# A turn's small matmul tiles in one cluster, with TensorE's program aligned to its fetch blocks

## The chip, the cores and the metric

The kernel runs on one core of one Trainium2 chip. The metric is the device time of one execution in microseconds; lower is better.

## What is computed

A gated linear attention is followed by a gated state-space block. With B=4, H=8, S=768, D=48:

```python
for t in range(S):
    state = alpha[:, :, t, :, None] * state + np.einsum('bhd,bhe->bhde', k[:, :, t], v[:, :, t])
    y[:, :, t] = np.einsum('bhd,bhde->bhe', q[:, :, t], state)
x = y.transpose(0, 2, 1, 3).reshape(B, S, H * D)          # (4, 768, 384)
proj = x @ w_in                                            # w_in: (384, 1024)
val, gate = proj[..., :512], proj[..., 512:]
for t in range(S):
    h = exp(A_log) * h + val[:, t, :]
    ys[:, t, :] = h
out = (silu(gate) * ys) @ w_out                            # w_out: (512, 384)
```

Everything is computed in float32; `w_in`, `A_log` and `w_out` come as float64.

## The kernel before

The 3072 rows are cut into 12 chunks of 256, three for each batch. A turn n projects chunk n and does its output while the attention of chunk m = n+1 is finished and that of chunk m+1 is begun. The program order of each engine is written out by hand in the loop over n; there is no scheduler behind it, and every engine works its list in order. Turns 0 and 1 are special; from n=2 on the turns are alike.

The attention of a chunk has these parts. VectorE turns alpha, k and q (`turn`, L601), scans alpha to running products P and V (L636, L655), and scales k and q with them to `Zk` and `Zq` (L620, L611). These are the steps of `products`; `go(1)` issues the next one, and seven belong to a chunk. TensorE then works in tiles of 48 or 64 rows, four side by side: `scores` (L799) multiplies Zk and Zq; `masks` (L814, L815, L819, L821) takes the results out to `A0`, `AK` and `K0` with VectorE, ScalarE and GpSimd; `values(m, True)` and `values(m, False)` (L835) multiply v with the masked scores across and within 64-row halves; `states` (L867) makes each half's addition to the state, which ScalarE evicts to `dS` (L875) and GpSimd adds up to `sums` (L887, `add_up`); and `carried` (L848) multiplies q with the sums. `third` is carried, values and carried again, and `join` copies the result `y` to `yst` and `xT` (ScalarE, L961, L962, L967) and moves the pieces that change partitions with DMAs from SyncE and GpSimd (L964).

A float32 matmul shows as two passes of TensorE, each with a weight load of its own. A projection (`project`, L989) is six matmuls, so twelve passes, of 128x256 with full 128-row tiles; four of them make the 48 passes of a turn. Its first half feeds a scan on VectorE (L996), its second half a SiLU on ScalarE (L1007), and GpSimd multiplies both (L1009). The output (`output_parts`, L1072) uses a Strassen-like form with seven half-width products, 28 passes of 128x192; it is a generator, whose pieces the loop draws with `next(outs)`. Its sums of inputs are S1 to S4 (L1056 to L1061), and VectorE's three additions of results (L1100 to L1102) are its last piece, which the following turn draws.

PSUM has eight banks. Two pairs have names, s and y; the other four are taken in the order of a string of digits, `taken`, written by hand (`bank`). There is one buffer each for raw alpha, k and q: the load of the next chunk waits until the present one is turned. `check_w` looks at the exponents of the weights; its result, with other conditions, chooses at the end between the fast kernel and a general one, by a branch on every engine.

In a turn from n=3 on TensorE's order before is: four projections; `carried`, `values(m, False)`, `carried`; `scores(m+1)`; the output's 28 passes; `values(m+1, True)`, `states(m+1)`; the next turn's projections. The outer ones are large tiles, the others small.

Of the kernel before, what the change touches and what calls it, by code (L numbers as in the profile page):

```python
# [343 lines left out]
FLOOR = 1e-31  # L344


@with_exitstack
def fast(
# [128 lines left out]
    As, Ks = [A0, AK[:, :, :, D:]], [K0, AK[:, :, :, 0:L]]  # L477
# [184 lines left out]
    def products(m):  # L662
# [21 lines left out]
                 "23012301" "230132" "01230123" "012310" "23012301" "230132" "01230123" "012310"  # L684
                 "23012301" "230132" "01230123" "012310" "23012301" "230132" "01230123" "012310"
                 "23012301" "0132" "01320132" "0132")

    def bank(tag=None):
        if tag:
            return ps_at.tile([C, 512], FP32, tag=tag, name=tag)  # L690
        return ps_mm.tile([C, 512], FP32, tag=f"mm{next(taken)}", name="mm")
# [111 lines left out]
    def masks(m, cs=range(G), between=None):  # L803
# [9 lines left out]
        for c in range(G):  # L813
            nc.vector.tensor_mul(A0[:, c], sc[c][0][:, :, D:], mb.to_broadcast([C, 4, L]))  # L814
            nc.scalar.activation(AK[:, c], sc[c][1], AF.Copy)  # L815
        if between:
            between()
        t = AK.rearrange("p c h x -> p (c h) x")[:, :, D:]
        nc.gpsimd.tensor_mul(t, t, mb.to_broadcast([C, G * 4, L]))  # L819
        for c in range(G):  # L820
            nc.scalar.activation(K0[:, c, :, 0:D], sc[c][0][:, :, 0:D], AF.Copy)  # L821

    def values(m, across):

        v_sb = vs[m % NV]
        if across:
            ys[m] = [t.rearrange("p (e t) -> p e t", e=2) for t in bank_pair("y")]
        for c in range(G):
            for e in range(2):
                for h in range(2):  # L830
                    i = 1 - h if across else h
                    for s in range(2):
# [3 lines left out]
                                         v_sb[rows, c, 4 * i + p, :], As[i][rows, c, p, :],  # L836
# [15 lines left out]
    def states(m):  # L852
# [7 lines left out]
        for c in range(G):  # L860
            for p in range(4):
                for h in range(2):
                    if c < n[h]:
                        rows = ds(L * h, L)
                        for i in range(2):
                            to = st[h][ds(64 * i, D), c, p, :] if m else st[h][c][ds(64 * i, D), p, :]
                            nc.tensor.matmul(to, ((K0, dS[m % 2][1]) if m < NG else Ks)[i][rows, c, p, 0:D],  # L867
# [6 lines left out]
        for h in range(2):  # L874
            nc.scalar.activation(parts[h][:, 0:n[h], :, 0:D], st[h][:, 0:n[h]], AF.Copy)  # L875
# [100 lines left out]
    def project(n, cc, late=False, between=None):  # L976
# [14 lines left out]

        passes(order[:NK] if between else order)
# [82 lines left out]
    def output_parts(n):  # L1075
# [11 lines left out]
        yield  # L1087
# [125 lines left out]
    def second(m):  # L1213
        if m < N:
            values(m, True)
            states(m)
            add_up(m, (0, 1, 2))

    def third(m):
        if m < N:  # L1220
            carried(m, (1,))
            values(m, False)
            carried(m, (0, 2, 3))
            return join(m, [nc.sync, nc.gpsimd])

    late = (1,)
    for n in range(N):
# [37 lines left out]
        elif n == 1:  # L1265
# [29 lines left out]
            f2()  # L1295
            output(0)
# [8 lines left out]
        else:  # L1305
            if n == 2:
                first(m)
            if n - 1 not in late:
                go(1)
                if n == N - 2:  # L1310
                    check_w(5)
                next(outs, None)
                second(m)
                go(1)
                if n == N - 2:
                    check_w(0)
            else:
                go(1)
            f0 = project(n, 0)
            f0()  # L1320
            if n == N - 2:
                check_w(1)
            if n == 2:
                go(1)
            load_raw("a", n + 3, nc.sync)
            load_raw("k", n + 3, nc.sync)
            if n != 2:
                go(1)
# [3 lines left out]
            if n - 1 in late:  # L1332
                second(m)
            if n == 2:
                go(1)
# [10 lines left out]
            load_raw("q", n + 3, nc.sync)  # L1346
# [3 lines left out]
            f3 = project(n, 3)  # L1350
            f3()
            if m + 1 < N:
                go(1)
# [6 lines left out]
            rest = third(m)  # L1360
            if n < N - 1:
                outs = output_parts(n)
# [25 lines left out]
        if n == N - 2:  # L1388
            for _ in outs:
                pass  # L1390
# [55 lines left out]
```

## Time and profile before

| | us |
|---|---|
| median of 3 runs | 269.65 (269.63 to 269.8) |
| the profiled execution | 269.61 |
| its span, first to last instruction | 267.9 |
| TensorE (PE) busy | 262.4 |
| VectorE (DVE) busy | 236.9 |
| GpSimd (POOL) busy | 166.0 |
| ScalarE (ACT) busy | 111.9 |

PE are the matmul passes, PEld the weight loads that overlap them. In the chain of waits each line has its start, its length and the work, with the count of passes; ends of matmuls are modelled, so the border between two pieces stands a little behind the start of the next piece's first pass. In a timeline a bracket at the end of a line gives the engine's idle time before it and what ended it. In a stretch of time the columns are its length, then the busy time of PE, PEld, DVE, ACT and POOL with their instructions, the granted clock, the DMA share and GB/s. TensorE's granted clock is 1.00 throughout.

### The profile page before, as it was taken

Reading aid. Unit: us, or ns where it says so; the run is one execution under the profiler, and the core shown is the slowest. Engines: PE = TensorE matmul, PEld = TensorE weight load, DVE = VectorE, ACT = ScalarE, POOL = GpSimd, SP = SyncE. Lnnn points to the kernel's source line nnn. Section 1 sums busy time; section 2 is a strip of 40 time slices with the busy share of each in tenths; the row PEclk is TensorE's granted clock in tenths of the full one; section 3 lists DMA queues with packets and bytes.
Section 4 is the critical chain, followed back from the end, with each engine's and each line's share of the span. In section 5 each row is a group of like instructions: output and inputs, shape, how many; then the busy total and the mean of one; then the engine's idle time right before and its main releaser. Section 6 shows DMA issues by size and latency. Waiting matters only on the chain.

```text
span 267.9 us, 10005 instructions
## 1 busy us (share of the span) xinstructions
PE 262.4 (98%) x4172; PEld 230.5 (86%) x4172; DVE 236.9 (88%) x326; ACT 111.9 (42%) x272; POOL 166.0 (62%) x186
## 2 busy tenths in 40 slices
PE   7999999999999999999999999999999999999994
PEld 5998889877688988988988988988988989988984
DVE  7979998996999999999999998999999998883462
ACT  4667766372242642532533524524524515214021
POOL 8221314084168997995985995996876986646010
PEclk9999999999999999999999999999999999999999
DMA  5948984896993669559697488569598501201101
GB/s 177 307 141 262 287 187 152 227 209 149 271 219 82 133 164 223 122 146 221 132 230 165 104 218 184 125 160 216 128 209 174 144 2 29 76 2 38 68 7 60
DMA packets 52304, 41.19 MB, mean 154 GB/s; under 512 B 27392, under 2 KB 50944, under 8 KB 52256
## 3 DMA queue, kind: packets, MB, share of 16 engines
q1 hardware_dynamic: 49472, 37.53, 57.8%
q0 software_dynamic: 1536, 2.20, 3.2%
q10 hardware_dynamic: 1248, 0.79, 1.1%
q8 instruction: 34, 0.56, 0.9%
q14 instruction: 14, 0.11, 0.1%
HBM read 32.54 MB, written 4.72 MB: 139 GB/s over the span
## 4 chain that ended last, share of the span: by engine, by line
PE 91%; DVE 2%; DMA 2%; issue 1%; ACT 1%; POOL 1%; ACTq 0%; DVEq 0%; POOLq 0%
PE mm L989 47%; PE mm L1072 18%; PE y L835 4%; PE y L848 4%; PE mm L1023 4%; PE s L799 4%; PE mm L799 3%; PE s L867 3%; DMA raw_q<-in_q_dram 2%; PE mm L708 1%; PE mm L704 1%; PE mm L703 1%; DVE P L636 1%; PE mm L751 1%; POOL w_in L557 1%
## 5 line engine op out<-in xcount | busy, mean ns | idle before, releaser
L989 PE MATMUL mm<-xT,w_in 128*128 128x256 f32 x576 | 129.2, 382 | 0.1
L989 PEld LDWEIGHTS mm<-xT,w_in 128*128 128x128 f32 x576 | 108.0, 190 | 15.8 <-POOL w_in L557 0.4
L1007 ACT ACTIVATE sg<-mm 128x256 f32<-128x256 f32 x48 | 18.4, 383 | 88.8 <-PE mm L989 84.4
L1009 POOL TENSOR_TENSOR f_last<-sg,hh 128x256 f32<-128x256 f32 x36 | 28.3, 794 | 26.1 <-ACT sg L1007 22.6
L887 POOL TENSOR_TENSOR sum<-sum,dS 128x192 f32<-128x192 f32 x30 | 39.7, 1325 | 3.0 <-ACT dS L875 1.4
L636 DVE TENSOR_TENSOR_SCAN P<-al,lower 128x1028 f32<-128x1028 f32 x12 | 30.7, 2562 | 0.3
L996 DVE TENSOR_TENSOR_SCAN hh<-a_dec,hh,mm 128x256 f32<-128x256 f32 x32 | 23.3, 729 | 8.3 <-PE mm L989 7.8
L655 DVE TENSOR_TENSOR_SCAN V<-al,ends 128x1028 f32<-128x1028 f32 x12 | 28.5, 2375 | 0.4
L964 POOL DMA_DIRECT2D xT<-yst x44 | 22.5, 517 | 5.1 <-ACT yst L961 3.7
L557 POOL TENSOR_TENSOR w_in<-w_in,wr 128x768 int32<-128x768 int32 x4 | 7.3, 1823 | 25.5 <-DVE wr L552 16.1
L1072 PE MATMUL mm<-wide,wr 128*128 128x192 f32 x120 | 23.0, 327 | 0.0
L1072 PEld LDWEIGHTS mm<-wide,wr 128*128 128x128 f32 x120 | 20.0, 190 | 0.0
L601 DVE STREAM_TRANSPOSE k<-raw_k 128x1024 f32<-128x1024 f32 x9 | 18.5, 2054 | 0.0
L601 DVE STREAM_TRANSPOSE q<-raw_q 128x1024 f32<-128x1024 f32 x9 | 18.3, 2030 | 0.0
L875 ACT ACTIVATE dS<-s 128x384 f32<-128x384 f32 (+1 forms) x18 | 7.4, 461 | 24.4 <-PE s L867 24.4
L1072 PE MATMUL mm<-w_out,f_last 128*128 128x192 f32 x80 | 17.4, 340 | 0.0
L819 POOL TENSOR_TENSOR AK<-AK,mask 128x512 f32<-128x512 f32 x9 | 13.7, 1522 | 5.9 <-ACT AK L815 5.7
L601 DVE STREAM_TRANSPOSE al<-raw_a 128x1024 f32<-128x1024 f32 x8 | 16.4, 2052 | 0.0
L620 DVE TENSOR_TENSOR Zk<-k,V 128x1024 f32<-128x1024 f32 (+1 forms) x14 | 16.0, 1146 | 0.3 <-ACT k L715 0.3
L611 DVE TENSOR_TENSOR Zq<-q,P 128x1024 f32<-128x1024 f32 (+1 forms) x14 | 15.7, 1120 | 0.0
L848 PEld LDWEIGHTS y<-Zq,sum 48*64 48x64 f32 x656 | 11.6, 134 | 3.5 <-issue 3.2
L835 PE MATMUL y<-A,v 64*64 64x64 f32 x352 | 14.5, 221 | 0.0
(196 smaller groups left out, 502.5 us busy)
## 6 DMA issues: line engine op xcount, KB each, us to landing
out_dram<-o_sb SPq DMA_DIRECT2D x23, 192.0 KB, 2.3
v<-in_v_dram SPq DMA_DIRECT2D x22, 192.0 KB, 4.1
raw_k<-in_k_dram SPq DMA_DIRECT2D x18, 184.0 KB, 5.2
raw_q<-in_q_dram SPq DMA_DIRECT2D x18, 184.0 KB, 5.4
raw_k<-in_k_dram SPq DMA_DIRECT2D x18, 176.0 KB, 5.4
raw_q<-in_q_dram SPq DMA_DIRECT2D x18, 176.0 KB, 5.4
wbits<-in_moe_w_in_dram SPq DMA_DIRECT2D x8, 384.0 KB, 4.9
raw_a<-in_alpha_dram SPq DMA_DIRECT2D x16, 184.0 KB, 3.9
```

The costliest lines, as they stand in the source:

```text
L601: nc.vector.transpose(out=by_runs(to).rearrange("p h c j -> p h j c"), in_=raws[name][:, 0:4 * ROW].rearrange("p (h j d) -> p h j d", h=4, ...
L636: nc.vector.tensor_tensor_scan(out=P, data0=al[:, 0:4 * GP], data1=lower.rearrange("p h t -> p (h t)"), initial=0.0, op0=ALU.mult, op1=ALU ...
L655: nc.vector.tensor_tensor_scan(out=V[:, ::-1], data0=al[:, 1:4 * GP + 1][:, ::-1], data1=ends.rearrange("p h t -> p (h t)")[:, ::-1], init ...
L799: nc.tensor.matmul(scs[m][c][i][ds(L * h, L), ds(p * (L + D), L + D)], Zk[rows, c, p, ds(h * L, L)], Zq[rows, u, p], start=True, stop=True ...
L835: nc.tensor.matmul(ys[m][i][ds(64 * s, 64), e, ds(c * C + h * L, L)], v_sb[rows, c, 4 * i + p, :], As[i][rows, c, p, :], start=across and ...
L848: nc.tensor.matmul(ys[m][i][ds(64 * s, 64), e, ds(u * L, L)], Ss[j][rows, p, :], Zqs[m % 2][rows, u, p, D:], start=False, stop=True, skip_ ...
L887: nc.gpsimd.tensor_add(Ss[j][:, :, 0:D], Ss[j - 1][:, :, 0:D], part)
L964: engines[n % len(engines)].dma_start(out=xT[to, a], in_=st[rows, i, e])
L989: nc.tensor.matmul((pv, pg)[vg], w_ins[cc][:, kk, vg, :], xT[:, kk, :], start=(kk == 0), stop=(kk == NK - 1))
L996: nc.vector.tensor_tensor_scan(out=hh, data0=a_dec[:, cc:cc + 1].to_broadcast([C, GC]), data1=pv, initial=prev_h[cc][:, GC - 1:GC] if n % ...
L1009: f = lambda: engine.tensor_mul(fs[n][cc], sg, hh)
L1072: nc.tensor.matmul(o, a[:, k], b[k] if type(b) is list else b[:, k], start=start and k == 0, stop=k == KC - 1, skip_group_check=True)
```

## The change

`scores(m+1)` moves directly behind the last projection, ahead of `carried`. `states(m+1)` and `values(m+1, True)` move from behind the output to directly behind `carried`, so that a turn has one cluster of small tiles instead of two; for m in `apart` (5 and 8), they stay behind the output. Because the y tiles of two chunks now overlap, those after the first batch's take rotating banks (the string has the letters a and b for the named y banks too), and `A0` and `AK` get second buffers in the place of the finished weight bits `wobits[0]`, whose check moves into turn 1; another check moves to the end of turn 9. GpSimd's mask is done in two halves. The eviction of states becomes a function called between pieces of the output. The steps of `products` shift by one place in the turn, the last scan and gate of a turn come behind the scaled q, and the raw loads move. Ahead of the third projection in turns 2 to 9 `addr_align(256, BLOCK_PLACE, max_nops=0)` places the next TensorE instruction at slot 212 of a block of 256 program slots of 64 bytes; the padding is jumped over by a branch.

```diff
+BLOCK_PLACE = 212
...
-    As, Ks = [A0, AK[:, :, :, D:]], [K0, AK[:, :, :, 0:L]]
+    spare_A = wobits[0].rearrange("p a n two -> p (a n two)").bitcast(FP32)
+    AKs = [spare_A[:, 0:G * 4 * (D + L)].rearrange("p (c h x) -> p c h x", c=G, h=4), AK]
+    A0s = [spare_A[:, ds(G * 4 * (D + L), G * 4 * L)].rearrange("p (c h x) -> p c h x", c=G, h=4), A0]
...
-                 "23012301" "230132" "01230123" "012310" "23012301" "230132" "01230123" "012310"
-                 "23012301" "230132" "01230123" "012310" "23012301" "230132" "01230123" "012310"
-                 "23012301" "0132" "01320132" "0132")
+                 "23012301" "23" "01" "23ba" "23ab23ab" "23" "ab" "2310"
+                 "23012301" "23" "23ba" "01" "23ab23ab" "23" "ab" "2310"
+                 "23012301" "23" "01" "23ba" "23ab23ab" "23" "2310" "ab"
+                 "23012301" "23" "01" "23ba" "23ab23ab" "23" "ab" "2310"
+                 "23012301" "2310" "23ab01ab" "0132")
...
         for c in range(G):
-            nc.vector.tensor_mul(A0[:, c], sc[c][0][:, :, D:], mb.to_broadcast([C, 4, L]))
-            nc.scalar.activation(AK[:, c], sc[c][1], AF.Copy)
-        if between:
-            between()
-        t = AK.rearrange("p c h x -> p (c h) x")[:, :, D:]
-        nc.gpsimd.tensor_mul(t, t, mb.to_broadcast([C, G * 4, L]))
-        for c in range(G):
+            nc.vector.tensor_mul(A0s[m % 2][:, c], sc[c][0][:, :, D:], mb.to_broadcast([C, 4, L]))
+            nc.scalar.activation(AKs[m % 2][:, c], sc[c][1], AF.Copy)
             nc.scalar.activation(K0[:, c, :, 0:D], sc[c][0][:, :, 0:D], AF.Copy)
+            t = AKs[m % 2][:, c, :, D:]
+            nc.gpsimd.tensor_mul(t, t, mb.to_broadcast([C, 4, L]))
...
+        if cc == 2 and 1 < n < N - 2:
+            nc.tensor.addr_align(256, BLOCK_PLACE, max_nops=0)
         passes(order[:NK] if between else order)
...
             f2 = project(n, 2)
             scaled_k(3, tk, V)
             f2()
+            check_w(4)
...
+                if m + 1 < N:
+                    go(1)
+                    load_raw("k", n + 3, nc.sync)
+                go(1)
                 next(outs, None)
-                second(m)
-                go(1)
...
             f0 = project(n, 0)
             f0()
+            go(1)
...
-            f3 = project(n, 3)
+            h3, f3 = project(n, 3, True)
+            if m + 1 < N:
+                go(1)
+            h3()
             f3()
             if m + 1 < N:
-                go(1)
+                scores(m + 1)
+            go(1)
+            if m + 1 < N:
+                masks(m + 1)
...
+            if m < N:
+                rest = third(m)
+                load_v(m + 2, nc.sync)
+                load_raw("q", n + 3, nc.sync)
+                if m + 1 < N and m not in apart:
+                    evict = states(m + 1)
+                    values(m + 1, True)
+                if n + 3 < N:
+                    load_raw("a", n + 4, nc.sync)
+                rest()
                 outs = output_parts(n)
                 next(outs)
+                if m + 1 < N and m not in apart:
+                    evict()
                 next(outs)
+                if m in apart:
+                    values(m + 1, True)
+                    states(m + 1)()
+                if m + 1 < N:
+                    add_up(m + 1)
+            if n == N - 3:
+                check_w(0)
```

More of the change, by code (lines that the diff above doesn't have):

```diff
@@ L1211, in first @@
             masks(m)
[L1213 to L1217, printed above, removed]
-    def third(m):
[L1220 to L1226, printed above, removed]
+    def third(m):
+        carried(m, (1,))
+        values(m, False)
+        carried(m, (0, 2, 3))
+        return join(m, [nc.sync, nc.gpsimd])
+    apart = (5, 8)
     for n in range(N):
```

82 lines of the change are left out of this document (29 added, 53 removed).

## The prediction

> **What bounds the kernel now.** I read the profile from the outside in: the page for the share of each engine, then the chain of waits in order of time, then the timelines of VectorE and ScalarE over one turn.
>
> ```profile
> span 267.9 us, 10005 instructions
> PE 262.4 (98%) x4172; PEld 230.5 (86%) x4172; DVE 236.9 (88%) x326; ACT 111.9 (42%) x272; POOL 166.0 (62%) x186
> PE 91%; DVE 2%; DMA 2%; issue 1%; ACT 1%; POOL 1%; ACTq 0%; DVEq 0%; POOLq 0%
> 113.89 0.04 PE s L867 x2
> 113.94 10.56 PE mm L989 x48
> 124.49 0.39 PE y L848 x16
> 124.89 0.47 PE y L835 x32
> 125.35 0.70 PE y L848 x48
> 126.05 0.77 PE s L799 x32
> 126.82 0.77 PE mm L799 x32
> 127.59 4.75 PE mm L1072 x28
> 132.34 0.62 PE y L835 x32
> 132.96 0.72 PE s L867 x64
> ...
> 249.07 10.36 PE mm L989 x48
> 259.44 4.99 PE mm L1072 x28
> ```
>
> TensorE is busy 98% of the span and holds 91% of the chain. The chain lines show turn n=4 whole: 48 passes of the projections (L989), a cluster of small tiles (carried, values, carried, scores), 28 passes of the output (L1072), a second cluster (values and states of the next step), and at once the next projection. Nothing else stands between them, so a gain has to come out of TensorE's own time, and a loss out of a wait that TensorE does not have today.
>
> VectorE is close behind. Here are turn 4 as a stretch, and then the vector operations of turn 5, whose projections begin at 133.68:
>
> ```profile
> 113.94:133.68 19.74, 19.74 (x333) 17.80 (x333) 19.01 (x21) 7.69 (x20) 16.45 (x17) 1.00 0.76 169
> ```
> ```profile
> 133.37 0.28 DVE L652 TENSOR_TENSOR ratio<-P,ends 128x4 f32<-128x4 f32 x1
> ...
> 136.27 0.73 DVE L996 TENSOR_TENSOR_SCAN hh<-a_dec,hh,mm 128x256 f32<-128x256 f32 x1
> 136.93 1.19 DVE L620 TENSOR_TENSOR Zk<-k,V 128x1024 f32<-128x1024 f32 x1
> 138.05 0.73 DVE L996 TENSOR_TENSOR_SCAN hh<-a_dec,hh,mm 128x256 f32<-128x256 f32 x1
> 138.70 2.02 DVE L601 STREAM_TRANSPOSE q<-raw_q 128x1024 f32<-128x1024 f32 x1
> 140.58 0.66 DVE L996 TENSOR_TENSOR_SCAN hh<-a_dec,hh,mm 128x256 f32<-128x256 f32 x1
> 141.18 1.17 DVE L611 TENSOR_TENSOR Zq<-q,P 128x1024 f32<-128x1024 f32 x1
> 142.98 0.75 DVE L996 TENSOR_TENSOR_SCAN hh<-a_dec,hh,mm 128x256 f32<-128x256 f32 x1 [0.63 <-PE mm L989]
> 143.64 2.04 DVE L601 STREAM_TRANSPOSE al<-raw_a 128x1024 f32<-128x1024 f32 x1
> 145.56 0.42 DVE L1060 TENSOR_TENSOR wr<-f_last,wr 128x256 f32<-128x256 f32 x1
> ...
> 146.78 0.41 DVE L814 TENSOR_TENSOR A<-s,mask 128x256 f32<-128x256 f32 x1
> ```
>
> VectorE works 19.01 of turn 4's 19.74 us, with its one idle place of note before the last scan of a turn. It is not the bound, but it has little to give, and the change makes TensorE ask for its results earlier.
>
> **The change part by part.**
>
> *Fewer changes between large and small tiles.* In the chain 48 projection passes with a small cluster ahead take 10.56 us, those of the last turn, with the output's large tiles ahead and behind, 10.36: entering large tiles costs 0.20. The 32 passes of values take 0.62 right behind large tiles and 0.47 inside a cluster: entering small tiles costs 0.15. A cluster less is worth 0.35. The second cluster joins the first in turns n=2, 3, 5, 6, 8 and 9 (in n=4 and 7 it stays behind the output, because m=5 and 8 are in `apart`). Six times 0.35 is 2.10 us. This is the whole possible gain: no pass is removed.
>
> *Scores directly behind the last projection.* Today the scores of the next step follow the carried products; now they come first, and need Zq at once. From the rows of turn 5: the last scan waits for its projection until 142.98, 9.30 us after the projections' start at 133.68; three projections of 10.36/4 = 2.59 earlier the first scan can start, 1.53 after the start. In the new order VectorE then runs a scan (0.66 to the next start), the scan for V with its small steps (133.37 to 136.27, 2.90), a scan (0.65), Zk (1.12), another scan (0.60), the turning of q (1.88) and Zq (1.17): 8.98 together, so Zq ends 10.51 after the projections' start. When could the scores start? The first small matmul of turn 4 starts at
>
> ```profile
> 124.42 0.46 PE L848 MATMUL y<-Zq,sum 48*64 48x64 f32 x16
> ```
>
> which is 10.48 after 113.94. Zq is 0.03 late, about 0.04 with the hand-over; I take 0.04 for turns 4, 5, 7 and 8. In turns 3, 6 and 9, first of a batch, the scans have no carried-in value and are shorter, so I take nothing. Both ends: nothing at all, or 0.3 if Zq takes 1.44 as once in the row below. In turn n=2 VectorE has no idle place before Zq at all, and there the wait is plain:
>
> ```profile
> 67.77 1.44 DVE L611 TENSOR_TENSOR Zq<-q,P 128x1024 f32<-128x1024 f32 x1
> ...
> 84.34 1.18 DVE L611 TENSOR_TENSOR Zq<-q,P 128x1024 f32<-128x1024 f32 x1
> ```
> ```profile
> 85.26 0.39 PE y L848 x16
> ```
>
> Zq ends at 85.52 and the small tiles of turn 2 begin about 85.19 (their chain piece at 85.26 less the 0.07 between piece and start in turn 4): 0.33, with the hand-over 0.35 lost.
>
> *States inside the cluster.* They write the bank from which VectorE masks the scores, so they wait for the first mask (L814). Behind Zq VectorE has a scan (0.66) and the turning of alpha (1.92, 143.64 to 145.56), then the mask (0.41): 10.51 + 2.99 = 13.50 after the start. TensorE arrives after 10.56 of projections, 0.15 of entry, 1.54 of scores and, in the turns without a first carried chunk (n=5, 8), 1.18 of carried and values (0.39 + 0.47 + 0.70, less the entry's 0.15 and 16 passes at 0.70/48): 13.43, so 0.07 late, or 0.05 once the scores have waited; twice 0.05. In the other turns 0.23 more carried work lies ahead and hides it. Values come 0.72 later and find both masks done; GpSimd's mask, now in two halves, has those 1.5 us as cover.
>
> *The output behind an unemptied y.* The y tiles of two steps now overlap, so they share the rotating banks. In turns 4 and 7 the third output product takes the bank of the second y tile at once, which ScalarE empties with two copies to yst and two to xT:
>
> ```profile
> 126.15 0.60 ACT L961 ACTIVATE yst<-y 128x512 f32<-128x512 f32 x1 [1.18 <-DMA raw_q<-in_q_dram]
> 126.64 0.59 ACT L962 ACTIVATE yst<-y 128x512 f32<-128x512 f32 x1
> ...
> 129.41 0.76 ACT L967 ACTIVATE xT<-y 48x256 f32<-48x256 f32 x2
> ```
> ```profile
> 128.27 1.46 PE L1072 MATMUL mm<-wide,wr 128*128 128x192 f32 x8
> ```
>
> Carried ended at 126.05 and yst began 0.10 later; two copies at 0.49 and 0.76 for the other two make 1.84. The third product starts about 0.65 into that last row, 128.92, which is 1.33 behind the end of the small tiles at 127.59. So it waits 0.50 in each of two turns: 1.00. In the merged turns states and values (over 1.3 us) lie between, and the bank is free. The bounds are 0 (if another bank is free) and 0.5.
>
> *The branch and the fetch.* Eight aligned branches, in n=2 to 9. What a branch costs:
>
> ```profile
> L1412 PEldq COMPARE_BRANCH  x1: 3837/3837/3837, 255.4 to 255.4; - x1
> ...
> L1412 DVEq COMPARE_BRANCH  x1: 84/84/84, 260.7 to 260.7; - x1
> ```
>
> TensorE's sequencer spent 3.84 us on the only branch of before, beginning at 255.4, and the matmuls behind it still ran at 259.44 without a hole in the chain: the sequencer runs some 4 us ahead in large tiles. What shows is at most 4.99 - 4.75 = 0.24 for 28 passes. So a branch costs between 0 and 0.24; I take 0, since this jump is of the DVE row's kind, short and inside one block (the first two projections end near slot 80 or 110, the target is 212). Fetches:
>
> ```profile
> q8 instruction: 34, 0.56, 0.9%
> ```
>
> 34 packets for 8344 weight loads and matmuls is one for about 245, hence one per 256-slot block. Each packet took 0.9% x 16 x 267.9 / 34 = 1.13 us. From slot 212 two projections of 24 slots end at 260; the merged clusters have 240 passes at most, with their weight loads 480 instructions, and end at 740. So borders lie 4 slots ahead, once in the middle, and 28 slots behind. A block of small tiles lasts about 2.5 us (the 320 instructions of the present cluster take 3.10), above 1.13 by 1.4 for the start of a fetch. I price it at 0. The Trainium skill (Runtime: NRT & Kernel Launch, Instruction fetch mechanics) holds that a floor of about 20 cycles per instruction hides fetches; by that the alignment buys nothing and the sum stays. The trace neither shows nor excludes it: no hole of before is a fetch's, but no cluster of before is as long.
>
> *Moves that I cost at nothing.* The weights' check that moves into turn 1 adds two reductions to VectorE just ahead of a scan that waits anyway:
>
> ```profile
> 65.05 0.75 DVE L996 TENSOR_TENSOR_SCAN hh<-a_dec,hh,mm 128x256 f32<-128x256 f32 x1 [2.47 <-PE mm L989]
> ```
> ```profile
> L568 DVE TENSOR_REDUCE wmax<-wobits 128x1 f32<-128x768 f32 x2 | 1.9, 944 | 0.0
> ```
>
> Two of 0.94 fit into 2.47. The other check goes to the end of turn 9, where no step of a later chunk is left for VectorE. Loads of q and alpha now queue on SyncE behind the xT moves and the v load; k goes ahead of the output's stores. Each is wanted some 10 us later, against landing times of about 5, so I expect no wait, and fewer transfers beside the cluster's fetches. ScalarE's evictions of states move behind s1's copy; the sums that need them are read a turn later.
>
> *Sum.* -2.10 + 0.35 + 4 x 0.04 + 2 x 0.05 + 1.00 = -0.49 us. The profiled execution took 269.61 (span 267.9 and 1.7 around it), 0.04 under the median of 269.65. 269.61 - 0.49 = 269.12, so 269.1.
>
> **The rivals.**
>
> *The gain comes through.* If the third output product finds its bank free and the short waits vanish, -2.10 + 0.35 = -1.75: 267.9. For it: every small wait is within 0.1 us of nothing. Against it: ScalarE's order is fixed by the program. Half way, with half the bank wait, is 268.6. Chance 0.28 for this and what lies half way.
>
> *VectorE takes over (slower).* From the first scan to Zq nothing may slip: each 0.1 us there is 0.1 us of TensorE in every turn. If GpSimd's work falls beside it as in the row where Zq took 1.44, the scores wait 0.3 in seven turns, 2.1 in place of 0.16, and the states 0.2 more in two: -0.49 + 1.94 + 0.4 = +1.85, 271.5; half of it, 270.5. It decides above some 0.1 us of mean slip. For it: 19.01 of 19.74 busy. Against it: GpSimd has no work of the last gate yet while Zq runs. Chance 0.20.
>
> *The branch breaks the fetch (slower).* The Trainium skill's same section says that a taken branch out of the loaded window waits for a fetch. As a mechanism here: each of eight branches shows the 0.24 above, +1.9, 271.0. The jump stays in its block, so 0.10.
>
> *The merging is eaten exactly.* With the upper waits of two or three places, within 0.2%: 0.06.
>
> **How the numbers follow.** The forecast as such has 0.36 and its own range is 268.5 to 269.7. A measurement of this kernel can tell about 0.2%, 0.54 us, from no change; the forecast lies just on that border, so its chance is split: 0.16 faster, 0.18 same, 0.02 slower. With the first rival faster gets 0.44; with the eaten gain same gets 0.24; with the two slow ones slower gets 0.32. The range takes the full gain nearly whole and half to most of the slow cases: 268.0 to 271.0.
>
> **What would show it.** Right: in merged turns one cluster of 4.3 us, projections of 10.36 to 10.4 because large tiles lie ahead, and turns of about 19.4; turn 2 unchanged; in turns 4 and 7 a hole of 0.5 before the third output product, released by the xT copy; waits of TensorE for Zq of at most 0.1. Wrong: scores waiting over 0.2 in most turns (VectorE's chain), a hole of issue inside the cluster at its middle or at the third projection (fetch or branch), or turns 4 and 7 at their old 19.74 (no bank wait).

## The result, and the profile after

| | before | after |
|---|---|---|
| median, us (4 runs each) | 269.73 (269.63 to 269.84) | 284.0 (282.76 to 286.55) |
| ratio | | 1.054, 95% interval 1.047 to 1.062 |
| the profiled execution, us | 269.61 | 286.55 |

The change makes the kernel 5.4% slower; I had forecast 269.1 in a range from 268.0 to 271.0. The profiled execution is the slowest of the four. Medians here and below are of all executions, ratios of those not over 1.5% above their kernel's fastest, which leaves out three of the nine of e17 alone. The rows of the page of after that answer to those shown of before:

```profile
span 284.5 us, 10039 instructions
PE 266.3 (94%) x4172; PEld 233.1 (82%) x4172; DVE 234.3 (82%) x326; ACT 112.2 (39%) x272; POOL 145.1 (51%) x195
PE 61%; DVE 24%; issue 6%; DMA 3%; ACT 2%; SPq 1%; DVEq 0%; ACTq 0%
```

TensorE has the same 4172 passes, but holds 61% of the chain instead of 91%. VectorE now has 24%, and "issue", time in which the engine waits for nothing that the profile shows, has 6%. The chain of waits of turn 3 shows both at once (start, length, work; `...` stands for 0.02 us of issue):

```profile
106.60 2.04 DVE q L613
...
108.66 1.24 DVE Zq L623
109.89 0.14 issue
110.03 1.00 PE s L816 x32
111.03 0.77 PE mm L816 x32
111.79 0.23 PE mm L862 x16
112.02 0.47 PE mm L849 x32
112.49 0.22 PE mm L862 x13
112.71 0.62 issue
113.33 0.73 PE mm L862 x34
```

Before Zq ended, the scores could not start (the rows down to 110.03). Then, in the middle of the cluster, between two carried passes (L862), TensorE stands still with nothing to wait for. The view of waits groups both kinds (engine, tile and line, what it waited for: us in total, times, longest):

```profile
PEld y L862 <- issue: 5.3, 7, 1.2
PE s L816 <- DVE Zq L623: 4.1, 8, 0.9
PEld mm L862 <- issue: 3.3, 4, 1.0
```

From the passes' starts in the timeline I put the turns together. From the first projection of turn 2 to that of turn 10 before took 158.73 us and after 172.28, so 13.55 more. Of this, holes in the middle of the cluster are 8.15 (0.80 to 1.23, one in each of the eight turns). Scores that wait for Zq are 4.6 beyond the normal entry into small tiles (0.25 to 1.0 in each turn). The third output product of turns 4 and 7 waits 0.51 each. The saved switches are -2.1. That makes 11.7; the remaining 1.9 is spread over waits of at most 0.22, half of it in the output, and the switches save somewhat less than 2.1. Another 3.0 us stands ahead of turn 2, whose projections start at 76.11 instead of 73.09; most of the other profiles have nothing like it (last section).

### The profile page after: what moved, and what is told of

It is laid out like the page before. It is cut to its first block, busy times and chain, and to the rows that moved or that the text cites. A ratio compares the mean times of both kernels' runs of the same rounds, so it can differ in the third digit from the quotient of the medians.

```text
span 284.5 us, 10039 instructions
## 1 busy us (share of the span) xinstructions
PE 266.3 (94%) x4172; PEld 233.1 (82%) x4172; DVE 234.3 (82%) x326; ACT 112.2 (39%) x272; POOL 145.1 (51%) x195
## 4 chain that ended last, share of the span: by engine, by line
PE 61%; DVE 24%; issue 6%; DMA 3%; ACT 2%; SPq 1%; DVEq 0%; ACTq 0%
PE mm L1005 18%; PE mm L1090 14%; DVE q L613 6%; DVE V L667 4%; DVE Zq L623 4%; PE y L1005 4%; DVE hh L1014 3%; PE s L816 3%; PE mm L816 3%; PE y L1090 3%; PE y L862 2%; PE s L881 2%; PE mm L725 2%; DMA raw_q<-in_q_dram 2%; PE y L849 2%
## 5 line engine op out<-in xcount | busy, mean ns | idle before, releaser
L1005 PE MATMUL mm<-xT,w_in 128*128 128x256 f32 x456 | 103.6, 382 | 0.0
L1005 PEld LDWEIGHTS mm<-xT,w_in 128*128 128x128 f32 x456 | 85.5, 190 | 12.2 <-issue 0.5
L1027 POOL TENSOR_TENSOR f_last<-sg,hh 128x256 f32<-128x256 f32 x36 | 37.7, 1049 | 42.1 <-DVE hh L1014 21.2
L1005 PE MATMUL y<-xT,w_in 128*128 128x256 f32 x120 | 27.5, 379 | 0.0
L1005 PEld LDWEIGHTS y<-xT,w_in 128*128 128x128 f32 x120 | 22.8, 190 | 3.1
L569 POOL TENSOR_TENSOR w_in<-w_in,wr 128x768 int32<-128x768 int32 x4 | 7.3, 1820 | 26.5 <-ACT wr L556 9.6
L903 POOL TENSOR_TENSOR sum<-sum,dS 128x192 f32<-128x192 f32 x30 | 18.7, 624 | 2.0
L1090 PE MATMUL mm<-wide,wr 128*128 128x192 f32 x88 | 17.2, 327 | 0.3 <-issue 0.3
L816 PEld LDWEIGHTS s<-Zq,Zk 48*64 48x64 f32 x384 | 9.7, 133 | 8.1 <-PE y L1005 3.2
L816 PE MATMUL s<-Zq,Zk 48*64 48x112 f32 x384 | 11.9, 261 | 4.1 <-DVE Zq L623 4.1
L1090 PEld LDWEIGHTS mm<-wide,wr 128*128 128x128 f32 x88 | 14.7, 190 | 0.6 <-issue 0.6
```

The source lines that it names most:

```text
L816: nc.tensor.matmul(scs[m][c][i][ds(L * h, L), ds(p * (L + D), L + D)], Zk[rows, c, p, ds(h * L, L)], Zq[rows, u, p], start=True, stop=True ...
L903: nc.gpsimd.tensor_add(Ss[j][:, :, 0:D], Ss[j - 1][:, :, 0:D], part)
L1005: nc.tensor.matmul((pv, pg)[vg], w_ins[cc][:, kk, vg, :], xT[:, kk, :], start=(kk == 0), stop=(kk == NK - 1))
L1027: f = lambda: engine.tensor_mul(fs[n][cc], sg, hh)
L1090: nc.tensor.matmul(o, a[:, k], b[k] if type(b) is list else b[:, k], start=start and k == 0, stop=k == KC - 1, skip_group_check=True)
```

## The experiments

The kernel before ran beside each; its medians were 269.7 to 270.1. All times are medians. "Order" below means a changed order of VectorE's steps, shown at e5. Only in e1, e10 and e11 did the time fall into the range of the theory that I named first; e9 came out below it, all others above.

**One part at a time: e1 to e4.** e1 takes the branch out:

```diff
-        if cc == 2 and 1 < n < N - 2:
-            nc.tensor.addr_align(256, BLOCK_PLACE, max_nops=0)
```

> Theory T1 (a wait plus a fetch): TensorE's sequencer stops at the wait for Zq ahead of the scores; only when it goes on does it ask for the next block of 256 program slots, which is usable about 3.3 us later; the first 252 instructions of the cluster take 2.46 us, so TensorE stands in the middle of the cluster for 0.8 to 1.2 us in every turn, 8.1 us in all, and 4.6 us more at the waits for Zq. Without the alignment the borders fall elsewhere in every turn: the Zq waits stay, some turns have their hole near the cluster's start or end and some none, so 278 to 285 us, with holes of differing sizes and places. T2 (the branch itself does the harm, by breaking the fetch): the holes in the clusters go, about 275 us. T3 (VectorE is the bound alone, holes are its consequence): no change, 284.

It took 282.93, ratio 1.049 (1.047 to 1.051). The Zq waits stay; the holes go to other places. In its view of waits they lie at the carried products, at values and at states:

```profile
PEld mm L862 <- issue: 2.7, 3, 1.2
PEld y L849 <- issue: 2.3, 5, 1.0
PEld s L881 <- issue: 1.7, 3, 0.7
```

So the branch is not the harm; the alignment only decides where the hole is. e2 moves the borders 16 slots:

```diff
-BLOCK_PLACE = 212
+BLOCK_PLACE = 228
```

> Slot 228 in place of 212: the border ahead of the cluster lies 20 slots ahead of the scores, inside the third part of the last projection, in place of 4. T1: the sequencer passes this border some 3 us before TensorE gets to the scores, so the fetch of the middle block is not held up by the wait for Zq; the hole in the middle goes in all eight turns (8 us), the Zq waits stay: 275 to 277 us. T2 or a fetch that is too slow at any place: the hole only moves by 16 instructions and stays 0.8 to 1.2 us: 283 to 285.

281.52, 1.042 (1.039 to 1.045). The middle hole is gone from turn 3 on. What comes instead is a wait that the Zq waits and holes had hidden: states, and in turns 4 and 7 the first output product, wait for ScalarE's K, which stands behind VectorE's mask and its turning of alpha. Turns 2 and 9 have a hole in the output, of 0.9 and 0.4.

```profile
PE mm L1090 <- ACT K L833: 1.6, 2, 0.8
PEld s L881 <- ACT K L833: 1.8, 7, 0.4
```

e3 puts VectorE's scan for V ahead of the first projection's scan:

```diff
+                go(1)
             if n == N - 2:
                 check_w(5)
             f0 = project(n, 0)
             f0()
-            go(1)
+            if n == 2:
+                go(1)
```

> From turn 3 on the step of the scan for V goes ahead of the first projection's scan on VectorE, where VectorE stood idle 0.87 us for that projection. T1: Zq comes 0.4 to 0.9 us earlier, the Zq waits fall from 4.6 to about 1.5 us, and the sequencer gets past the wait earlier against TensorE by what is then left over, so the holes in the middle shrink too: 277 to 280 us. A theory in which the fetch's hole has nothing to do with the wait: only the Zq part goes, 280.5 to 281.5. T3: as T1's lower part.

281.46, 1.044 (1.041 to 1.046). The passes of the scores wait 1.5 us for Zq in all instead of 4.1, the holes are nearly as they were (7.7 us in all). That is the time of my rival, a hole that has nothing to do with the wait; but the scores still wait in every turn. e4 lets the scores read a Zq that has long been done; its scores are those of a wrong chunk.

```diff
-        Zk, Zq = Zks[m], Zqs[m % 2]
+        Zk, Zq = Zks[m], Zqs[(m + (m > NG)) % 2]
```

> The scores of a chunk read the scaled q of the chunk before (so they are not the reference's), and so wait for Zk only, which is ready over 3 us earlier; all work of all engines stays. T1: without the wait the sequencer runs ahead over the border; both the Zq waits (4.6) and the holes in the middle (8.1) go: 270 to 273 us. If the hole is the fetch's own and does not depend on the wait: only 4.6 go, and the holes stay at 0.8 to 1.2: 279 to 280 us.

279.11, 1.034 (1.032 to 1.036). This too is the rival's 279 to 280, and yet not as the rival has it: no wait for Zq is left and the middle holes fall from 8.15 to 2.2 us (0.44, 1.23 and 0.55 in turns 2, 4 and 8), but most of the gain is lost to the next wait:

```profile
PEld s L881 <- ACT K L833: 4.0, 10, 1.1
```

**Without VectorE's waits: e5 to e8.** e5 changes the order so that no wait for Zq or for a mask is left: the edit of e3, the turning of q ahead of the third projection's scan, and the masks ahead of the turning of alpha.

```diff
-            go(1)
+            go(2)
             f2 = project(n, 2)
...
-            go(1)
...
                 scores(m + 1)
+                masks(m + 1)
             go(1)
-            if m + 1 < N:
-                masks(m + 1)
```

> Three moves in VectorE's order alone, at the old slot 212: V ahead of the first projection's scan, the turning of q ahead of the third projection's scan, the masks ahead of the turning of alpha. T1 (the hole in the cluster comes from the wait for Zq, which holds the sequencer): Zq is there about 1 us before TensorE needs it, so the Zq waits go (4.6 us) and the holes in the middle shrink from 0.8-1.2 to 0-0.2 us (7 us): 271 to 274 us. T2 (the fetch is too slow at slot 212 whatever the wait): Zq waits go, holes stay: 278 to 280.

277.73, 1.028 (1.025 to 1.032). The waits are gone but for 0.2 in turn 2; the holes are not, which is nearly what the rival T2 said. The passes of turn 3 in its timeline:

```profile
105.69 1.00 PE L816 MATMUL s<-Zq,Zk 48*64 48x112 f32 x32
106.51 0.95 PE L816 MATMUL mm<-Zq,Zk 48*64 48x112 f32 x32
107.27 0.41 PE L862 MATMUL mm<-Zq,sum 48*64 48x64 f32 x16
107.50 0.65 PE L849 MATMUL mm<-wobits,v 64*64 64x64 f32 x32
107.97 0.40 PE L862 MATMUL mm<-Zq,sum 48*64 48x64 f32 x13
109.39 0.74 PE L862 MATMUL mm<-Zq,sum 48*64 48x64 f32 x34 [1.02 <-issue]
```

32+32+16+32+13 passes with their weight loads are 250 instructions; the next weight load, which still ran, and the semaphore instruction ahead of the scores make 252: the hole is at the block border, 252 slots into the cluster. e6 and e7 have the same order with slot 228; e7 also merges turns 4 and 7, with the banks of the other merged turns. e8 has slot 228 and of the order only the masks.

```diff
-BLOCK_PLACE = 212
+BLOCK_PLACE = 228
...
-    apart = (5, 8)
+    apart = ()
```

> The same moves and slot 228. T1: both guards against the hole at once; no hole in the middle, 0 to 1 us under the run with slot 212: 270.5 to 273. T2: with the holes gone by the slot and the waits by the order, this and not the run before it falls to 271-273.

> As the run before, but turns 4 and 7 merged like the others (nothing in apart, the banks in the same rotation). They save a pair of switches (0.35) and the wait of the third output product for the y bank (0.5) each, 1.7 us; but their clusters of 512 instructions reach over the border behind, 2.2 us after the one in the middle, against 3.3 us for a fetch: a hole of up to 1.1 us at the end of each. T1: between -1.7 and +0.5 us against the run before.

> Slot 228 as in e2_place_228 (281.5 us) and the masks ahead of the turning of alpha, the Zq order as in the change. What was left in e2_place_228 were waits of states and of the output for ScalarE's K0, which waits for VectorE's mask behind the 1.9 us turning of alpha. If that is the cause, these 4 to 5 us go and the Zq waits (4.6) stay: 276 to 278. If VectorE is simply out of time, the delay only moves to the next wait for VectorE: 280 to 282.

e6 took 275.69, 1.022 (1.015 to 1.028); e7 277.11, 1.025 (1.022 to 1.028); e8 279.27, 1.034 (1.030 to 1.037). In e6 no hole is left in the middle, but in turns 2, 3, 5, 8 and 9 one of 0.6 to 0.9 stands behind the cluster, where the third border lies 12 slots into the output. The chain of turn 3 of e6:

```profile
111.95 0.86 PE mm L1090 x4
112.81 0.49 issue
113.30 4.06 PE mm L1090 x24
```

In e7 the cluster of turns 4 and 7 has 512 instructions, so the third border lies inside it, and the holes are 2.06 and 1.72. e8 keeps its Zq waits and loses only those for K. The masks are worth 2.3 us (e2 to e8), the Zq waits 3.6 (e8 to e6), and the fetch of the program most of the rest.

**Is it the border's place? e9 to e12.** e9 and e10 add only the branch of e1's diff to the kernel before, at slots 212 and 228.

> The kernel before, in its old order with two clusters, and only the aligning branch of the change added to it at the same place (slot 212 ahead of the third projection in turns 2 to 9): a border four slots ahead of the first cluster, the next one 252 instructions into it. Theory F (the harm is the fetch: a block is usable some 3.5 us after the border ahead of it is crossed, and 256 slots of small tiles last 2.2 to 2.5 us): a hole of 0.8 to 1.2 us in the middle of the first cluster of each of the eight turns although nothing is merged, so 269.9 + 8 x 1.0 = 276 to 279. Rival M (a cluster of 480 instructions is what hurts, by its length or by what waits at its head): the branch costs next to nothing here, 269.7 to 270.5.

> The same with BLOCK_PLACE 228: the border 20 slots ahead of the first cluster, the next one 236 instructions into it, the third one after 172 slots of output and second cluster. Theory F: the block for the middle of the cluster is asked for in the large tiles and is there in time, no hole in turns 3 to 9; turn 2 may pay up to 1.6 us where its jump crosses a border: 269.9 to 271.5. Rival B (each branch costs time by itself, whatever the border's place): as much as at slot 212, so 276 to 279 if that one loses, or both about 270.

e9 took 270.42, 1.003 (1.001 to 1.006), and e10 271.09, 1.006 (1.004 to 1.007). My theory F said 276 to 279 for e9, and it fell. Here is turn 4 of e9 in the chain:

```profile
125.39 0.39 PE y L849 x16
125.78 0.47 PE y L836 x32
126.25 0.70 PE y L849 x48
126.94 0.77 PE s L800 x32
127.72 0.77 PE mm L800 x32
```

The cluster starts four slots behind a border and crosses the next one after 252 instructions, like that of e5, and there is no hole (of the eight turns only turn 3 has one, of 0.37). The view of DMA shows why. In the 4.3 us ahead of this cluster (121 to 125.32) the middle block's packet has already begun:

```profile
q1 hardware_dynamic: 731, 0.94, 106.9%
q8 instruction: 1, 0.02, 1.9%
```

In the 4 us ahead of e5's cluster (101.7 to 105.7) there is none; it comes in the next 2.4 us:

```profile
q1 hardware_dynamic: 677, 0.86, 109.7%
```
```profile
q8 instruction: 1, 0.02, 2.5%
```

And e5's TensorE sequencer passes the semaphore of the first scores at 105.4, 0.04 behind the end of Zq and only 0.3 ahead of the scores, although no pass waits for it; in all turns of after and e5 it passes 0.04 behind the end of Zq. In e4, with the old Zq, it passes 3.4 us ahead of the scores of turn 4 at 127.5:

```profile
L816 PEldq EVENT_SEMAPHORE  x1: 51/51/51, 105.4 to 105.4; - x1
```
```profile
L816 PEldq EVENT_SEMAPHORE  x1: 51/51/51, 124.1 to 124.1; - x1
```

So the lead counts. In the old order nothing holds the sequencer ahead of the cluster (carried products come first), and it crosses the border while the large tiles are still running. In the new order it is held at the scores until Zq ends, just in time for the passes but too late for the fetch.

But a lead alone is not enough. In this very turn of e4 the packet begins 1.4 us behind the scores, and the hole is there:

```profile
129.97 0.22 PE y L862 x13
130.19 1.02 issue
```

Raw loads and the output's stores filled the DMA engines from the semaphore to shortly before the packet, which came 4.8 us after it. In turn 9 of e4, where no load is left, it came 1.1 us after, and the turn has no hole. Loads are not what made the holes of after, though: its turns 2 and 9 have idle DMA engines ahead of the cluster and holes of 0.98 and 0.80, and in all its eight turns the packet comes 0.95 to 1.24 us behind the semaphore, loads or not. Here are turn 4 of e4, turn 9 of e4 and turn 9 of after, each as a stretch ahead of the packet (the last but one column is the DMA share):

```profile
124.00:128.50 4.50, 4.50 (x57) 3.81 (x59) 4.47 (x5) 0.77 (x2) 2.14 (x3) 1.00 1.07 243
```
```profile
228.50:232.40 3.90, 3.90 (x19) 3.22 (x17) 3.68 (x3) 0.38 (x1) 2.04 (x3) 1.00 0.02 4
```
```profile
235.00:238.50 3.50, 3.33 (x16) 2.61 (x15) 3.46 (x4) 0.46 (x2) 1.41 (x2) 1.00 0.00 0
```

e11 and e12 look for the point: e11 is e5 with slot 220, e12 e5 with 216 and other banks in turns 4 and 7 (turn 4's are shown).

```diff
-                 "23012301" "23" "23ba" "01" ...
+                 "23012301" "23" "2301" "ba" ...
```

> The changed kernel with VectorE's steps reordered as before (V ahead of the first scan, turning of q ahead of the third one, masks ahead of turning alpha) and BLOCK_PLACE 220: borders 12 slots ahead of the cluster, 244 into it, 20 slots into the output. Theory F with a request that depends on the border alone: no hole in the middle, and the one behind the cluster shrinks by eight slots of output, from about 0.7 to about 0.4: 275.7 - 6 x 0.3 = 273 to 274.5, less if turn 2's jump no longer crosses a border (-1.2). If the request comes 12 slots or more behind the border, the middle holes of slot 212 are back: 277 to 278.

> The same with BLOCK_PLACE 216 and with other PSUM banks in the turns of m = 5 and 8: the output's third and fourth product get banks 0 and 1, the y tiles the named pair. Taken away: the third product's wait of 0.5 us in turns 4 and 7. Theory F: no hole in the middle if the request comes within 8 slots of the border, 0.3 behind the cluster, so 275.7 - 6 x 0.4 - 1.1 = 271 to 273 (1.2 less if turn 2's jump stays in its block). If the request comes later than that, holes of about 1.1 in the middle: 276 to 277.

274.35, 1.015 (1.011 to 1.020), and 278.54, 1.034 (1.028 to 1.039). With borders 20 slots ahead of the held instruction (e6) the block comes in time, with 12 (e11) mostly, with 8 (e12) in two turns of eight, with 4 (e5) never. Why the request for the block does not go out before the hold with 4 slots is not shown. Turns of e11 and e12 without a hole took 19.41 us: 0.32 less than the 19.73 of before, against my 0.35. The mechanism of the gain was real.

**A cluster with a head that nothing holds: e13 to e15.** In e13 the first carried product, 32 instructions, goes ahead of the scores; e14 adds the order, the banks and slot 204; e15 is e14 without the alignment.

```diff
-        carried(m, (1,))
+        if m <= 2 or m + 1 == N:
+            carried(m, (1,))
...
+                carried(m, (1,))
                 scores(m + 1)
```

> The changed kernel with one part put differently: carried(m, (1,)), eight small products that wait for nothing, goes ahead of scores(m+1) instead of behind it, so that it heads the cluster. Theory L (lead): a border costs nothing where TensorE's sequencer runs ahead of the passes, and it runs ahead only where nothing holds it; scores wait for a Zq that comes just in time, so the sequencer begins the cluster with no lead and asks for the middle block only then. With 32 instructions ahead that nothing holds, the block is asked for in the large tiles: the middle holes (8.2 us over eight turns) are gone, the Zq waits shrink by up to 0.3 each (-2): 273 to 277. Rival (the hole belongs to slot 212 and to 252 small instructions in a row, lead or not): the holes stay, 281 to 283.

> The version to which theory L points: that head, VectorE's steps reordered (V ahead of the first scan, turning of q ahead of the third one, masks ahead of turning alpha), banks 0 and 1 for the third and fourth product in the turns of m = 5 and 8, and BLOCK_PLACE 204, which puts borders 4 instructions into the cluster, 260 into it and 36 into the output. Theory L: no hole in a turn from n=3 on; merged turns of 19.4 us against 19.5 to 19.7, turns 4 and 7 of 19.7, turn 2 of 21 to 22.5: 267.5 to 269.5. Rival (three borders a turn cost 0.8 us somewhere wherever they lie): 273 to 276.

> The same without the alignment, so that borders fall anywhere. Theory L: the first border is asked for in time wherever it falls in the large tiles or the head; a border that falls into the first half of the scores or behind them is not, so some turns have holes of 0.3 to 1.2 and some have none: 269 to 273. Rival (with the head in place the alignment does nothing): the same as with it within 0.5 us.

e13 took 280.02, 1.035 (1.030 to 1.039). The middle holes fall from 8.15 to about 2.5 us, as theory L has it, but the time misses its 273 to 277 by 3: scores still wait 0.3 to 0.8 for Zq in most turns, states now wait for K (2.5 us in all), and the profiled execution lost 2.4 ahead of turn 2.

e14 took 272.75, 1.009 (1.006 to 1.012); its profile (270.38, its fastest run) has no hole over 0.33. e15 took 275.56, 1.019 (1.016 to 1.022), with four holes of 1.1 to 1.2 where borders fall unluckily.

In this order the alignment is worth about 3 us; in the old one (e9) it is worth nothing.

**What is left: e16 to e18.** e16 is e14 with slot 212, relabelled banks against waits of 0.2 at the next turn's projections, and `rest()` behind the first output products in turns 4 and 7.

```diff
-                rest()
+                if m not in apart:
+                    rest()
                 outs = output_parts(n)
                 next(outs)
+                if m in apart:
+                    rest()
```

e17 moves one load:

```diff
+                load_raw("q", n + 3, nc.sync)
                 rest = third(m)
                 load_v(m + 2, nc.sync)
-                load_raw("q", n + 3, nc.sync)
```

> The version with the head in place and nothing held, with its last visible losses taken away: BLOCK_PLACE back at 212, so that the middle block is asked for earlier (the border four instructions ahead of the cluster instead of four behind its start; in the profile of slot 204 its packet began only 0.3 to 1.8 us ahead of the cluster, and the runs of that kernel lay from 270.4 to 273.8); the banks relabelled so that the next turn's first projection does not wait 0.21 us for VectorE's second output addition (four turns, 0.8); join's last copies behind the first two products in the turns of m = 5 and 8, where the third product waited for ScalarE's copy (2 x 0.25). Theory L: 268 to 270, and a spread between runs of under 1.5. Rival (the spread comes from something other than a block that is just in time, or VectorE's chain takes what TensorE gains): 271 to 273.

> The version of e16 with one load moved: the raw q of a later chunk is asked for ahead of the carried products and the moves of xT, some 5 us earlier, when the DMA engines are idle. In the traces so far the raw loads keep them over 90% busy from the start of a turn until about 1 us behind the cluster's start, and where no load is left (turn 9) the middle block's packet begins 3 to 5 us ahead of a cluster whose head is not held, against 0.3 to 2.8 us elsewhere. Theory D (the loads also delay the packets of the fetch): the loads end earlier, the packets of turns 4 to 8 begin 1 us or more earlier, and the runs' spread of 3.6 us shrinks; 270 to 272, less a turn 2 of 22.6 us that may fall to 21.2 or not. Rival (the loads have nothing to do with it): packets and spread as in e16, 272 to 273.5; or worse, 274, if the moves of xT come late behind the load.

272.67, 1.010 (1.007 to 1.013), and 273.98, 1.010 (1.007 to 1.014). Both miss the 268 to 270 and 270 to 272 of my theories. From turn 3 on neither profile has a hole. In turns 3 to 9 the packet of the middle block begins 0.4 to 3.4 us ahead of the cluster in e16 and 1.5 to 3.1 in e17; without turn 9, where no load is left, the mean goes from 1.3 to 2.3. So the raw loads, which keep the DMA engines over 90% busy until the cluster starts, delay the fetch as well. Of the 4.0 us that e17's profiled execution is behind that of before, 2.65 stand in turn 2, most of them in one hole of its chain:

```profile
88.39 0.22 PE y L862 x13
88.61 2.56 issue
```

Turn 2's branch is the only one that starts from a place that nothing aligned. e18 puts another branch into turn 1:

```diff
+        elif cc == 3 and n == 1:
+            nc.tensor.addr_align(256, 20, max_nops=0)
```

> The version of e17 with one more aligned branch, in turn 1 ahead of its last projection (slot 20). Turn 2's branch is the only one that does not start from an aligned place, and in e17's trace turn 2 has the only hole left (2.76 us in the middle of its cluster; turn 2 takes 23.71 us against 21.05 before, turns 3 to 9 take 137.93 against 137.69). The new branch puts turn 2's own branch at slot 193, 19 slots ahead of its target and in the same block; turn 1's has large tiles ahead of it. Theory J (a jump into a block that is not loaded costs the lead, and with it the middle block): turn 2 falls to 21.0 to 21.4, the runs come together at 269.8 to 270.8, no faster than before, because VectorE's chain sets the rest. Rival (turn 2's hole is the raw loads' beside it, not the jump's): turn 2 stays at 22.5 to 23.7, 272.5 to 274; or the new branch costs as much in turn 1.

272.15, 1.006 (1.003 to 1.009). Turn 2 falls from 23.71 to 21.20 (before 21.05), as theory J has it, but the median misses its 269.8 to 270.8. TensorE's sequencer spent this on the new branch (L1011) and on the eight others:

```profile
L1011 PEldq COMPARE_BRANCH  x1: 2727/2727/2727, 58.1 to 58.1; - x1
```
```profile
L1009 PEldq COMPARE_BRANCH  x8: 181/185/204, 79.6 to 214.3; - x8
```

The new branch took 2.7 us, here covered by large tiles, the others 0.2 each. In e17 turn 2's branch took 0.2 as well (0.214), so that jump did not itself stand still; that it costs the lead is concluded from turn 2's time alone. The profiled execution (270.47) has all turns near those of before. Turn 3 as a stretch (length, then busy PE, PEld, DVE, ACT, POOL):

```profile
94.37:113.78 19.41, 19.41 (x318) 17.82 (x317) 18.16 (x22) 7.78 (x20) 17.04 (x20) 1.00 0.76 176
```

Only turns without a short wait reach 19.41. Turn 5 takes 19.50 (before 19.51). Turns 4, 6 and 7 take 19.86 to 19.93. In turn 5 VectorE's Zk takes 1.75 us (1.19 before) and Zq ends 0.3 behind the cluster's start:

```profile
139.21 1.75 DVE L632 TENSOR_TENSOR Zk<-k,V 128x1024 f32<-128x1024 f32 x1
143.39 1.18 DVE L623 TENSOR_TENSOR Zq<-q,P 128x1024 f32<-128x1024 f32 x1
```

Turns 3 to 9 sum to 137.97, those of before to 137.69: with every hole gone from turn 3 on, what the switches give is taken back. That VectorE's chain and small bank waits do it is read from this one trace, not tried. No merged version beat the kernel before. What stays open is that e18's runs fall into two groups, five at 270.05 to 270.6 and seven at 272.1 to 273.1; the profile is of the first, so what the second loses is not shown.

## Why the prediction was wrong

**The fetch at nothing.** This is the step that failed, 8.15 of the 13.55 us. I compared a block of small tiles, "about 2.5 us", with 1.13 for the packet and the 1.4 that this leaves for its start, called it covered, and did not carry the near balance into the range. In the traces of after and e5 the middle block's packet begins 0.5 to 1.4 us behind the first scores, takes 0.9 to 1.4, and the block is used 1.2 to 1.6 after its end, a time for which the sum had no term: 2.8 to 3.7 us, against the 2.5 that 252 instructions last. More important, I wrote that the sequencer "runs some 4 us ahead in large tiles" and used it for the branch, but did not ask whether it still does at a cluster whose first instruction waits. "A hole of issue inside the cluster at its middle" was on my list of what would show me wrong. The Trainium skill (Runtime: NRT & Kernel Launch, Instruction fetch mechanics) calls the cost of a block border mostly hidden; e9 agrees in all turns but one (0.37 us), after and e5 do not, with 0.3 to 1.2 us a border.

**Zq at 0.51 in all; 4.6 measured.** The chain was the right one, its terms were too short. The last steps of VectorE's timeline in turn 4 of after:

```profile
127.45 2.03 DVE L613 STREAM_TRANSPOSE q<-raw_q 128x1024 f32<-128x1024 f32 x1
129.52 1.23 DVE L623 TENSOR_TENSOR Zq<-q,P 128x1024 f32<-128x1024 f32 x1
```

Zq starts 2.06 behind the start of q's turning, because it needs its end, where I took the 1.88 to the next start; the V block with its small steps took 3.02 instead of 2.90 (122.00 to 125.02). From the first scan at 121.34 to the end of Zq at 130.75 it is 9.40 us, against my 8.98, and the scores follow 0.14 later, where I had put 0.01. At zero slack, each tenth came through: 0.59 in this turn. Turns 5 and 8 wait longer (0.84), and turns 3, 6 and 9, which I had put at nothing, 0.25. The rival "VectorE takes over" was right in kind, and e3 and e5 show it; at 271.5 it was too small, with 2.45 of waits for Zq (2.1, and 0.35 in turn 2) and the fetch still free.

**States and the mask, 2 x 0.05.** Hidden in after; e2 and e4 uncovered it, up to 1.1 at a time. The wait is for K, which ScalarE takes only after VectorE's mask, and that stands behind the turning of alpha.

**Right.** The switches: turns without a hole are 19.41, 0.32 shorter. The third output product: 0.51 in each of turns 4 and 7, as priced. The branch inside its block: 0.18 to 0.22 of the sequencer and nothing of the passes (e9). Turn 2 was wrong in two ways: 0.35 became 1.0 for Zq and another 1.0 for the hole.

**The weights' check at nothing** held in most profiles (projections of turn 2 at 72.8 to 73.8). In e4 and e16 they started at 74.5, in after, e13 and e15 at 76.11, 75.46 and 74.89. In the last three TensorE waited 1.1 to 1.6 us for a gate of VectorE's (L1027) ahead of turn 2: with 1.9 us of the 2.47 spent on the check, a VectorE that falls behind earlier in the turn has little cover left. I had not priced the loss of that cover.

## What to carry to other kernels

Here a run of short instructions used up a block of the program in 2.5 us, sooner than the next one came, so the fetch was paid for by the sequencer's lead. A semaphore that fired just in time took that lead away and cost up to 1.2 us a border even where no pass seemed to wait; full DMA engines used up the lead where there was one. Before a dense cluster is put behind a wait, put work ahead of it that nothing holds, and check that the block borders fall there. And price a chain with zero slack by its ends, not by the starts of the next instructions.

## What the runs showed that I had not expected

A block border costs nothing or a microsecond, depending on how far ahead of a held instruction it lies: 4 slots were too few in all eight turns (e5), 20 enough from turn 3 on (e2, e6 to e8).

The raw loads and the program's fetch share the DMA engines: one load moved 5 us earlier brought the fetch forward by 1 us on average (e16, e17, one trace each).

The same VectorE instruction has two durations. The second of two conversions of the weights (L564) took 2.25 us in the profile of after and 2.26 in that of e13, 0.60 to 0.63 in all others. What differs is GpSimd's work on the weights (L569). In after it begins 0.44 us ahead, and the conversion ends 0.47 behind its end:

```profile
54.35 2.22 POOL L569 TENSOR_TENSOR w_out<-w_out,wr 128x768 int32<-128x768 int32 x1 [6.93 <-ACT wr L556]
```
```profile
54.79 2.25 DVE L564 TENSOR_SCALAR wr<-wobits 128x768 uint16<-128x768 uint16 x1
```

In e13 it is the same, 0.25 ahead and 0.48 behind; in the others GpSimd begins 0.06 us ahead at most, or is not there (e15). No run moved the two against each other, so the cause is read from the traces only.

Of the 3.0 us ahead of turn 2 in after, 1.3 are there already at 31.4 us, where the scores of turn 0 begin (30.1 in before), and 0.5 is a hole of issue among the carried products at 56.3. The long conversion can account only for the rest, the 1.1 us that TensorE waits for VectorE's gate at 71.5.
